# Batch 0's group sums of queries and keys on TensorE, batch 1's values left unsummed, and a new order of the head

## The chip, the core and the metric

One core of a Trainium2 chip. The time is the device time of one execution in microseconds (us), the median of several runs. TensorE (PE) multiplies, VectorE (DVE), ScalarE (ACT) and GpSimd (POOL) do the elementwise work, and SyncE (SP) issues the DMAs.

## What is computed

```
q, k, v: (4 batches, 8 heads, 576 positions, 64)
q_d, k_d, v_d = means of q, k, v over groups of 4 positions      # 144 positions
out = softmax(q_d k_d^T / 8) v_d, each row repeated 4 times
    + softmax(q k^T / 8, only |i - j| < 4) v
x   = out as (2304 tokens, 512)
h   = x @ w_in;  g = h * sigmoid(1.702 h);  x = g @ w_out        # 2048 wide
h   = x @ w2_in; g = max(0.01 h, h);        out = g @ w2_out     # 2048 wide
```

Everything is float32 outside. Weights come as float64 bits and are made float32 on the chip.

## The kernel before

**Jobs.** Attention is cut into 16 jobs, one for a batch and a pair of heads: jobs 0 to 3 are batch 0, 4 to 7 batch 1 and 8 to 15 the late ones. A job has a coarse part (over the 144 group sums) and a band part (within 3 positions). Its steps have short names. q, k, va, vb, vh are loads. `Qd` and `Kd` sum the queries and keys over groups of four on VectorE (pool4, L325). `Sd` makes the coarse scores on PE (L434), `Mxd` their maxima and the negated, scaled maxima on VectorE (L441, L445), `Exd` three exponentials on ScalarE (L451), `Rcd` and `Mud` the division. `S0` and `S1` are the band scores of the two heads (L346, L351), `M0`/`M1` their maxima (L398), `N0`/`N1` the negation (L402, VectorE), `E0`/`E1` five exponentials each (L407), `Rc` and `Mu` the division. `T0`/`T1` transpose the coarse weights on PE (L461), `C0`/`C1` copy them out of PSUM on ScalarE (L151). `U0`/`U1` transpose the band weights (L528), `D0`/`D1` copy them out. `Vd` multiplies the coarse weights with the values (avd, L509), `Od` copies the product out, `Y0`/`Y1` multiply the band weights with the values (L568), `X0`/`X1` add both parts (L599).

**Values of the coarse part.** For batch 0, Vd needs no group sums: it runs over all four members of each group, two parts of the positions times four members times two heads, 16 matmuls of 144 columns. For batch 1, POOL first sums the values over the groups (`Va0`, `Va1`, `Vb0`, `Vb1`, pool_v, L338), and Vd is 4 matmuls.

**Layers.** The tokens are cut into blocks of 512 and four times 448. A unit (j, m) is block j and hidden slice m of 16. `L.u` is 12 matmuls (L735), `Gt`, `Gd`, `Gh`, `Gl` the gate on ScalarE, VectorE, ScalarE and POOL or VectorE, and `M.u` 12 matmuls (L780). Each operand is split into a high and a low float32r half, and three products are made. Units 0 and 1 are cut by input rows, `h0.kc` and `h1.kc`, so that they can begin as soon as one pair of heads is done (`xh`, `xl` split the input).

**Weights.** `w.n` loads half a slice, `wF`, `wL`, `wS`, `wB` turn its bits into float32 (VectorE; wF mostly on ScalarE), `wH` and `wO` make the high and low halves.

**The order.** The steps up to unit 13 stand in a list written out by hand (ORDER, L49). Every engine takes its steps in the order of the list, and so does SP its DMAs; a token's tail @A, @V or @G names ScalarE, VectorE or POOL in place of the usual engine. `z3.14` means 14 matmuls of 512 columns on zeros, into PSUM bank acc3: they do no work, and like every user of the bank they wait until what stood in it before has been read. acc0, acc1 and acc2 hold batch 0's S0, S1 and Sd, and acc3 holds Vd's product. After the list a loop runs the other units with the late jobs' steps between them.

Of the kernel before, what the change touches and what calls it, by code (L numbers as in the profile page):

```python
# [27 lines left out]
def attn_moe_kernel(ctx: ExitStack, tc, qT_d, kT_d, vh_d, vg_d, w1a, w2a, w1b, w2b, outT):  # L28
# [20 lines left out]
    ORDER = """  # L49
        w.2 wF.2 wL.2 wS.2 k.0 Kd.0 wB.2 wH.2 q.0 Qd.0 z3.14 S0.0 M0.0 S1.0 M1.0 va.4 Va0.4 Va1.4 w.0 wF.0@A Sd.0  # L50
        Mxd.0 Exd.0 wO.2 wL.0 N0.0 E0.0 N1.0 wS.0 Rcd.0 Mud.0 wB.0 wH.0 wO.0 k.1 q.1 z3.9 S0.1 Qd.1 Kd.1 M0.1
        w.3 wF.3@A wL.3 q.2 Sd.1 Mxd.1 wS.3 E1.0 Rc.0 Exd.1 vb.4 Vb0.4 wB.3 wH.3 wO.3 Vb1.4 Mu.0 Rcd.1 Mud.1
        N0.1 E0.1 T0.0 C0.0 T1.0 C1.0 q.4 k.4 z3.1 S.4 A1.4 k.2 va.1 w.1 wF.1@A S1.1 M1.1 A0.4 Qd.2 Kd.2 Mx.4
        Sb.4 z3.4 S0.2 M0.2 w.5 vb.7 wF.5@A Qd.4 Sd.2 Mxd.2 Exd.2 U0.0 D0.0 wL.5 N1.1 Kd.4 T0.1 k.3 z3.6 Sd.4
        wS.5 Rcd.2 Mud.2 wL.1 E1.1 Mxd.4 Exd.4 T1.1 C1.1 q.3 wS.1 N0.2 E0.2 wB.5 wH.5 wB.1 vb.2 Rc.1 Mu.1 Rcd.4
        Mud.4 q.5 vb.0 k.5 z3.5 S.5 Qd.5 A1.5 Qd.3 A0.5 Kd.3 z3.6 U1.1 D1.1 S1.2 T0.2 Kd.5 w.7 M1.2 wH.1 C0.1
        wO.5 Vb0.7 U1.0 D1.0 wO.1 Mx.5 Sb.5 N1.2 Sd.3 S0.3 M0.3 Mxd.3 T1.4 wF.7@A wL.7 va.0 T1.2 w.4 wF.4@A wL.4
        w.6 wF.6@A wS.7 wS.4 N0.3 wB.7 wB.4 E1.2 Rc.2 Mu.2 Ex.5 Exd.3 Rcd.3 Mud.3 C0.2 T0.4 C0.4 z3.4 S1.3 Vd.0
        M1.3 vh.0 Y0.0 k.6 va.6 va.5 vb.1 vh.4 C1.2 Od.0 X0.0 U0.1 D0.1 E0.3 wH.7 wO.7 C1.4 Ex.4 Y1.0 vh.1 va.2
        vh.2 w.12 vb.3 Vd.1 Od.1 w.9 X1.0 xh.0 wL.6 xl.0 N1.3 E1.3 wS.6 Sm.5 wB.6 Sm.4 Rc.4 Mu.4 Rc.5 Sd.5 Mxd.5  # L60
        T0.3 C0.3 Vd.4 Od.4 wF.9@A wH.4 wO.4 va.3 q.6 Vd.2 Y1.1 X1.1 h0.0 h1.0 U0.2 D0.2 T1.3 w.14 vh.3 Kd.6
        Va0.5 Va1.5 Exd.5 Rc.3 C1.3 Y0.1 U1.2 D1.2 X0.1 Qd.6 U1.4 D1.4 wL.9 Od.2 wH.6 xh.1 Y1.2 Y0.2 X1.2 Mu.3
        U1.3 D1.3 U0.3 D0.3 X0.2 wF.12@A xh.2 wS.9 wB.9 U0.4 D0.4 xl.1@V wO.6 xl.2 Y1.4 Vd.3 wH.9 wO.9 Od.3 Y0.3
        X0.3 Y1.3 X1.3 xh.3 h0.1 wL.12 xl.3@V wF.14@A wL.14 wS.12 wS.14 wB.12 L.2 Gt.2 Gd.2 wH.12 wO.12@V Gh.2
        Gl.2@V vb.5 Vb0.5 Rcd.5 Mud.5 w.8 wF.8@A wL.8 h1.1 h1.2 h1.3 Gt.1 Gd.1 Gh.1 wB.14 wS.8 wB.8 wH.8 Gl.1@V
        Mu.5@V L.3 wO.8 h0.2 h0.3 Y0.4 Gt.0 Gd.0 Gh.0 X0.4 w.19 wF.19@A w.15 wH.14 X1.4 Gl.0@V wL.19 Vb1.5 L.6
        wF.15@A Va0.6 wL.15 wS.19 wB.19 Gt.3 wO.14@V wS.15 wB.15 T0.5 T1.5 C0.5 w.10 wF.10@A wL.10 wS.10 wH.19
        wO.19 M.0 M.1 C1.5 Vd.5 Gd.3 Gh.3 Gl.3 wB.10 wH.10 wO.10 Va1.6 Sd.6 Mxd.6 M.2 L.4 Od.5@V va.7 w.16 Gt.6
        Gd.6 wF.16@A wL.16 wS.16 Exd.6 w.11 wF.11@A Rcd.6 Gh.6 wL.11 wS.11 wB.11 wH.11 wB.16 wH.15 Gl.6@V wO.15
        S.6 A0.6 A1.6 Mx.6 Mud.6 Sb.6 wO.11@V Gt.4 Gd.4 wH.16 wO.16@V w.22 Gh.4 Gl.4@V wF.22@A wL.22 vh.5 w.13  # L70
        wF.13@A wL.13 vb.6 w.20 wF.20@A wL.20 wS.20 wS.13 M.3 U1.5 D1.5 U0.5 D0.5 wB.13 wH.13 wO.13 L.5 wS.22
        Gt.5 wB.20 wH.20 Gd.5 Gh.5 Gl.5 Ex.6 wB.22 wH.22 wO.22 L.7 q.7 Qd.7 k.7 Kd.7 S.7 A1.7 wO.20 Sm.6 Gt.7
        Gd.7 M.4 w.18 wF.18@A wL.18 wS.18 wB.18 Gh.7 Gl.7@V wH.18 wO.18 Rc.6 A0.7 Mx.7 Sb.7 w.17 wF.17@A wL.17
        L.8 Gt.8 Gd.8 M.5 M.6 Y0.5 t.23 w.24 X0.5 Gh.8 Gl.8@V Vb0.6 w.26 wF.26@A wL.26 wS.17 wS.26 wB.26 Y1.5
        L.9 Gt.9 wH.26 T1.6 C1.6 w.28 wB.17 Gd.9 Gh.9 L.10 X1.5 Sd.7 Ex.7 wO.26 Mu.6@V wH.17 Gl.9@V wO.17 M.7
        M.8 Sm.7 Gt.10 Gd.10 Rc.7 wF.24@A wL.24 wS.24 wF.28@A wL.28 wB.24 w.21 wF.21@A wL.21 wS.21 Mxd.7 wS.28
        wB.21 wB.28 wH.24 Gh.10 Gl.10@V Vb1.6 U0.6 D0.6 Exd.7 Rcd.7 Va0.7 wH.28 L.11 Gt.11 Gd.11 T0.6 C0.6 U1.6
        D1.6 Gh.11 wO.24 Mu.7@V Mud.7 wO.28@V M.9 w.23 wF.23@A wL.23 wH.21 Vd.6 Od.6 vh.6 Y1.6 w.25 wF.25@A w.27
        X1.6 Va1.7 Gl.11@V wS.23 wB.23 wO.21@V Vb1.7 wL.25 wS.25 wB.25 wF.27@A wL.27 wH.23@V wO.23 L.12 Gt.12
        Gd.12 T0.7 C0.7 T1.7 L.13 t.25 wH.25 wO.25@V C1.7 w.29 w.31 Y0.6 X0.6 wS.27 U0.7 D0.7 Gh.12 wF.29@A  # L80
        wL.29 M.10 U1.7 D1.7 Vd.7 Od.7 wB.27 wH.27 wO.27 Gl.12@V wS.29 Gt.13 wF.31@A Gd.13 Gh.13 Gl.13 wB.29
        vh.7 Y0.7 X0.7 w.30 wF.30@A Y1.7 X1.7 wL.31 M.11 wS.31 wL.30 wB.31 wH.31 wH.29 wO.29 wS.30 wB.30 wH.30
        wO.30 wO.31 t.27
    """
# [838 lines left out]
```

## Time and profile before

| | |
|---|---|
| median of 3 runs | 914.37 us (914.04 to 915.45) |
| the profiled execution, its own time | 914.53 us |
| its span, first to last instruction | 912.7 us |
| granted TensorE clock | 1.00 |
| PE, DVE, ACT, POOL busy | 901.9, 405.5, 323.3, 338.4 us |

Busy time of PE is the union of matmuls whose ends are modelled, and it includes the matmuls on zeros. How much of it is work has to be read from the order of time: where a run of zeros (tile `idle`, L812) begins, and when the next matmul that does work starts.

### The profile page before, as it was taken

Reading aid. Unit: us, or ns where it says so; the run is one execution under the profiler, and the core shown is the slowest. Engines: PE = TensorE matmul, PEld = TensorE weight load, DVE = VectorE, ACT = ScalarE, POOL = GpSimd, SP = SyncE. Lnnn points to the kernel's source line nnn. Section 1 sums busy time; section 2 is a strip of 40 time slices with the busy share of each in tenths; the row PEclk is TensorE's granted clock in tenths of the full one; section 3 lists DMA queues with packets and bytes.
Section 4 is the critical chain, followed back from the end, with each engine's and each line's share of the span. In section 5 each row is a group of like instructions: output and inputs, shape, how many; then the busy total and the mean of one; then the engine's idle time right before and its main releaser. Section 6 shows DMA issues by size and latency. Waiting matters only on the chain.

```text
span 912.7 us, 14436 instructions
## 1 busy us (share of the span) xinstructions
PE 901.9 (99%) x5681; PEld 789.6 (87%) x5681; DVE 405.5 (44%) x723; ACT 323.3 (35%) x713; POOL 338.4 (37%) x322
## 2 busy tenths in 40 slices
...
GB/s 277 271 109 175 168 171 84 193 132 143 144 118 169 169 194 225 228 195 229 201 126 156 109 1 1 1 86 1 1 59 23 1 1 81 1 0 41 1 1 41
DMA packets 51908, 98.70 MB, mean 108 GB/s; under 512 B 11648, under 2 KB 25984, under 8 KB 51840
## 3 DMA queue, kind: packets, MB, share of 16 engines
...
q8 instruction: 45, 0.74, 0.3%
...
## 4 chain that ended last, share of the span: by engine, by line
PE 96%; DVE 2%; ACT 1%; DMA 1%; issue 0%; SPq 0%; ACTq 0%
PE h L735 44%; PE acc L780 44%; PE av L568 2%; PE avd L509 2%; PE sc L351 1%; PE scd L434 1%; DMA a<-qT 1%; PE pt L528 0%; ACT a L407 0%; DVE a L325 0%; PE pdt L461 0%; DVE stat L402 0%; DVE stat_d L441 0%; DVE t L175 0%; DVE t L179 0%
## 5 line engine op out<-in xcount | busy, mean ns | idle before, releaser
L735 PE MATMUL h<-xh,w 128*128 128x448 f32 (+1 forms) x1280 | 398.7, 373 | 0.0
L780 PE MATMUL acc<-gh,w 128*128 128x448 f32 (+1 forms) x1280 | 396.6, 371 | 0.0
L765 POOL TENSOR_TENSOR gl<-g,gh 128x448 fp32r<-128x448 f32 (+1 forms) x149 | 176.6, 1185 | 467.5 <-ACT gh L151 459.5
L735 PEld LDWEIGHTS h<-xh,w 128*128 128x128 f32 x1280 | 240.4, 188 | 27.7 <-issue 1.4
L780 PEld LDWEIGHTS acc<-gh,w 128*128 128x128 f32 x1280 | 240.4, 188 | 27.2 <-ACT g L753 1.8
L735 PE MATMUL h<-xl,w 128*128 128x448 f32 (+1 forms) x640 | 236.9, 370 | 0.0
L780 PE MATMUL acc<-gl,w 128*128 128x448 f32 (+1 forms) x640 | 236.8, 370 | 0.0
L761 DVE TENSOR_TENSOR g<-g,h 128x448 f32<-128x448 f32 (+1 forms) x80 | 50.8, 635 | 319.3 <-ACT g L760 319.3
L151 ACT ACTIVATE gh<-g 128x448 fp32r<-128x448 f32 (+1 forms) x160 | 94.3, 589 | 123.7 <-DVE g L754 64.8
L780 PEld LDWEIGHTS acc<-gl,w 128*128 128x128 f32 x640 | 120.2, 188 | 12.2
L735 PEld LDWEIGHTS h<-xl,w 128*128 128x128 f32 x640 | 120.2, 188 | 12.1
L760 ACT ACTIVATE g<-h 128x448 f32<-128x448 f32 (+1 forms) x80 | 44.4, 555 | 224.8 <-PE h L735 224.5
L754 DVE SCALAR_TENSOR_TENSOR g<-g,h 128x448 f32<-128x448 f32 (+1 forms) x80 | 50.6, 633 | 132.2 <-ACT g L753 131.7
L753 ACT ACTIVATE g<-h 128x448 f32<-128x448 f32 (+1 forms) x80 | 44.3, 554 | 156.2 <-PE h L735 147.8
L175 DVE SCALAR_TENSOR_TENSOR t<-s,t 128x512 uint32<-128x512 uint32 x64 | 64.1, 1006 | 1.5
L198 POOL TENSOR_TENSOR w<-t,w 128x512 fp32r<-128x512 f32 x25 | 33.6, 1349 | 50.1 <-ACT w L151 40.5
L179 DVE SCALAR_TENSOR_TENSOR t<-s,t 128x512 uint32<-128x512 uint32 x64 | 45.1, 711 | 1.5
L236 POOL TENSOR_TENSOR w<-b,w 128x1024 fp32r<-128x1024 f32 x16 | 38.5, 2404 | 7.9 <-ACT w L235 7.9
L378 POOL TENSOR_TENSOR P<-P,stat 128x320 f32<-128x320 f32 (+1 forms) x37 | 29.6, 818 | 10.5 <-DVE stat L417 9.9
L172 DVE TENSOR_SCALAR t<-t 128x512 uint32<-128x512 uint32 x64 | 30.8, 485 | 2.0 <-ACT t L151 0.8
L718 DVE TENSOR_TENSOR xl<-xf,xh 128x448 fp32r<-128x448 f32 (+1 forms) x27 | 20.5, 776 | 19.5 <-ACT xh L151 19.3
L151 ACT ACTIVATE xh<-xf 128x448 fp32r<-128x448 f32 (+1 forms) x40 | 22.9, 588 | 12.1 <-PE h L735 10.0
...
## 6 DMA issues: line engine op xcount, KB each, us to landing
...
```

The lines of the kernel that those rows point to most:

```text
L151: return nc.scalar.activation(out=out, in_=in_, func=AF.Copy, scale=scale)
L175: lambda: nc.vector.scalar_tensor_tensor(out=b, in0=bits[:, :, 1], scalar=0x80000000, in1=b, op0=ALU.bitwise_and, op1=ALU.bitwise_or,),
L179: lambda: nc.vector.scalar_tensor_tensor(out=b, in0=bits[:, :, 0], scalar=29, in1=b, op0=ALU.logical_shift_right, op1=ALU.bitwise_or,),
L198: lambda: on(G).tensor_tensor(out=lo, in0=t, in1=wt[e, m][:, 2 * i, :], op=ALU.subtract),
L236: nc.gpsimd.tensor_tensor(out=w[:, :, 1].bitcast(F32R), in0=t, in1=w[:, :, 0], op=ALU.subtract)
L735: nc.tensor.matmul(h, w[:, kc * P : (kc + 1) * P], xs[kc][part], start=kc == 0 and i == 0, stop=kc == KC - 1 and i == 2,)
L753: lambda: nc.scalar.activation(out=g, in_=h[:, :n], func=AF.Tanh, scale=0.5 * 1.702),
L754: lambda: nc.vector.scalar_tensor_tensor(out=g, in0=g, scalar=1.0, in1=h[:, :n], op0=ALU.add, op1=ALU.mult),
L760: lambda: nc.scalar.activation(out=g, in_=h[:, :n], func=AF.Copy, scale=0.01),
L761: lambda: nc.vector.tensor_tensor(out=g, in0=g, in1=h[:, :n], op=ALU.max),
L765: lambda: on(G).tensor_tensor(out=gl, in0=g, in1=gh.bitcast(F32), op=ALU.subtract),
L780: nc.tensor.matmul(acc[c][:, :n], w[:, cs], g, start=m == 0 and i == 0, stop=m == NM - 1 and i == 2)
```

## The change

P takes the place of Qd and Kd for jobs 0 to 3: 8 matmuls of PE with the identity as weights sum queries and keys into bank acc3, each reading every fourth column, and Pc copies the 2 x 144 sums out on ScalarE. Qd and Kd stay for the other jobs. The steps Va and Vb are gone from the list; batch 1's Vd runs over the four members, as batch 0's did, and four buffers instead of three hold the unsummed values. The negation of the band maxima, and that of the coarse maxima (now a step Nd of its own), can be put on ScalarE by @A, which the list does for N0 and N1 of every job of batch 0 and for every Nd but job 1's. The list is new throughout; below are its first lines, up to L.2.

```diff
     ORDER = """
-        w.2 wF.2 wL.2 wS.2 k.0 Kd.0 wB.2 wH.2 q.0 Qd.0 z3.14 S0.0 M0.0 S1.0 M1.0 va.4 Va0.4 Va1.4 w.0 wF.0@A Sd.0
-        Mxd.0 Exd.0 wO.2 wL.0 N0.0 E0.0 N1.0 wS.0 Rcd.0 Mud.0 wB.0 wH.0 wO.0 k.1 q.1 z3.9 S0.1 Qd.1 Kd.1 M0.1
-        w.3 wF.3@A wL.3 q.2 Sd.1 Mxd.1 wS.3 E1.0 Rc.0 Exd.1 vb.4 Vb0.4 wB.3 wH.3 wO.3 Vb1.4 Mu.0 Rcd.1 Mud.1
-        N0.1 E0.1 T0.0 C0.0 T1.0 C1.0 q.4 k.4 z3.1 S.4 A1.4 k.2 va.1 w.1 wF.1@A S1.1 M1.1 A0.4 Qd.2 Kd.2 Mx.4
-        Sb.4 z3.4 S0.2 M0.2 w.5 vb.7 wF.5@A Qd.4 Sd.2 Mxd.2 Exd.2 U0.0 D0.0 wL.5 N1.1 Kd.4 T0.1 k.3 z3.6 Sd.4
-        wS.5 Rcd.2 Mud.2 wL.1 E1.1 Mxd.4 Exd.4 T1.1 C1.1 q.3 wS.1 N0.2 E0.2 wB.5 wH.5 wB.1 vb.2 Rc.1 Mu.1 Rcd.4
-        Mud.4 q.5 vb.0 k.5 z3.5 S.5 Qd.5 A1.5 Qd.3 A0.5 Kd.3 z3.6 U1.1 D1.1 S1.2 T0.2 Kd.5 w.7 M1.2 wH.1 C0.1
-        wO.5 Vb0.7 U1.0 D1.0 wO.1 Mx.5 Sb.5 N1.2 Sd.3 S0.3 M0.3 Mxd.3 T1.4 wF.7@A wL.7 va.0 T1.2 w.4 wF.4@A wL.4
-        w.6 wF.6@A wS.7 wS.4 N0.3 wB.7 wB.4 E1.2 Rc.2 Mu.2 Ex.5 Exd.3 Rcd.3 Mud.3 C0.2 T0.4 C0.4 z3.4 S1.3 Vd.0
...
+        w.2 wF.2@A wL.2 wS.2 wB.2 q.0 k.0 z3.13 S0.0 M0.0 N0.0@A E0.0 S1.0 M1.0 w.3 wF.3 wL.3 q.1 P.0 Pc.0 z3.2
+        Sd.0 wS.3 wB.3 wH.3@V wO.3 k.1 P.1 S0.1 Mxd.0 k.4 Kd.4 N1.0@A E1.0 Rc.0 Mu.0 q.4 z1.3 S.4 Qd.4 A0.4
+        Nd.0@A Exd.0 Rcd.0 Mud.0 S1.1 M1.1 Pc.1 Sd.1 Mxd.1 w.1 wF.1@A wL.1 N1.1@A Nd.1 Exd.1 wS.1 wB.1 wH.1@V
+        w.7 wF.7@A wL.7 wH.2 wO.2 E1.1 Rcd.1 Mud.1 M0.1 N0.1@A Sd.4 Mxd.4 Nd.4@A A1.4 wS.7 wO.1@V E0.1 Rc.1 Mu.1
+        q.2 k.2 z3.10 P.2 Pc.2 T0.0 wB.7 z3.4 S0.2 M0.2 Sd.2 Mxd.2 Exd.4 Rcd.4 C0.0 Mud.4 N0.2@A w.0 wF.0@A wL.0
+        Nd.2@A U1.0 D1.0 T1.0 U0.0 S1.2 M1.2 wS.0 Exd.2 Rcd.2 Mud.2 va.0 w.5 wF.5@A wL.5 C1.0 q.3 D0.0 U0.1 D0.1
+        N1.2@A vb.0 T1.1 Vd.0 Od.0 k.5 Kd.5 E1.2 wS.5 k.3 P.3 Pc.3 wB.0 wH.0 wO.0 E0.2 T0.1 C0.1 wB.5 wH.5@V
+        wO.5 q.5 Qd.5 S1.3 S.5 A0.5 wH.7 A1.5 Mx.4 Sb.4 w.4 C1.1 Rc.2 Mu.2 z3.4 T0.2 C0.2 wF.4@A S0.3 M0.3
+        N0.3@A U1.1 M1.3 w.6 wF.6@A Ex.4 Sd.3 Mxd.3 Nd.3@A E0.3 Exd.3 D1.1 N1.3@A Mx.5 Sb.5 wL.6 va.2 vh.0 va.1
+        va.3 q.6 vb.1 vh.1 vb.3 vb.2 z3.5 Y1.0 X1.0 Y0.0 X0.0 xh.0 xl.0 wS.6 Sd.5 wL.4 wB.6 Rcd.3 Mud.3 Sm.4
+        Qd.6 w.9 vh.2 wS.4 Vd.1 E1.3 Rc.3 U0.2 T1.2 C1.2 D0.2 h0.0 wH.6 wO.6 Y1.1 Od.1 X1.1 U1.2 Ex.5 D1.2 Mxd.5
+        Nd.5@A Y0.1 X0.1 wB.4 w.14 vh.3 Vd.2 Od.2 Sm.5 wF.9@A wL.9 T0.3 T1.4 C1.4 C0.3 T1.3 C1.3 xh.1 h1.0 Mu.3
+        U0.3 D0.3 Y1.2 X1.2 Y0.2 X0.2 wO.7 wH.4 Exd.5 Vd.3 wF.14@A Od.3 U1.3 D1.3 Rc.4 wS.9 xl.1 Mu.4@V h1.1
+        h0.1 xh.2 wO.4@V w.12 T0.4 C0.4 Y0.3 X0.3 Y1.3 X1.3 wB.9 xh.3 xl.3@V xl.2@G wF.12@A wL.14 wL.12 U1.4
+        D1.4 U0.4 Rcd.5 wS.12 L.2 Gt.2 Gd.2 wS.14 wB.12 h0.2 h0.3 h1.2 h1.3 L.3 Gh.2 Gl.2@V D0.4 wH.12 wO.12@V
...
-    BUFS = {"stat": 4, "stat_d": 4, "P": 2, "pd": 2, "vg": 3}
+    BUFS = {"stat": 4, "stat_d": 4, "P": 2, "pd": 2, "vg": 4}
...
         def tiles(self):
-            self.qd = self.tile([P, SD], "qd")
-            self.kd = self.tile([P, SD], "kd")
-            if not self.first:
+            if self.first:
+                self.qkd = self.tile([P, 2, SD], "qd")
+                self.qd, self.kd = self.qkd[:, 0], self.qkd[:, 1]
+            else:
+                self.qd = self.tile([P, SD], "qd")
+                self.kd = self.tile([P, SD], "kd")
+            if self.late:
                 self.vd = self.tile([DK[0], 2, 2, D], "vd")
...
+        def pool_mm(self):
+
+            ps = self.ps_q = self.bank("acc3", "qk")
+            for i, x in enumerate((self.q[:, :S], self.kT[:, HALO : HALO + S])):
+                x = x.rearrange("p (g r) -> p r g", r=FACTOR)
+                for r in range(FACTOR):
+                    nc.tensor.matmul(
+                        ps[:, i * SD : (i + 1) * SD], ident, x[:, r], start=r == 0, stop=r == FACTOR - 1
+                    )
+
+        def pool_out(self):
+            copy(self.qkd, self.ps_q[:, : 2 * SD].rearrange("p (i g) -> p i g", i=2))
...
         def negate(self, h2):
             mx = self.stat[:, 0, :, h2]
-            nc.vector.tensor_scalar(out=mx, in0=mx, scalar1=-SCALE, scalar2=None, op0=ALU.mult)
+            copy(mx, mx, -SCALE, V)
...
             nc.vector.tensor_reduce(out=mx, in_=self.ps_d, axis=AX.X, op=ALU.max)
             if self.late:
-                nc.scalar.activation(out=mx, in_=mx, func=AF.Copy, scale=-SCALE_D)
-            else:
-                nc.vector.tensor_scalar(out=mx, in0=mx, scalar1=-SCALE_D, scalar2=None, op0=ALU.mult)
+                self.negate_d()
+
+        def negate_d(self):
+            mx = self.stat_d[:, 0]
+            copy(mx, mx, -SCALE_D, nc.scalar if self.late else V)
...
-            parts = [(kh, r) for kh in range(2) for r in range(FACTOR if self.first else 1)]
+            parts = [(kh, r) for kh in range(2) for r in range(1 if self.late else FACTOR)]
...
-                        v = self.vg[kh][:, h2, g, :] if self.first else self.vd[: DK[kh], kh, h2, :]
+                        v = self.vg[kh][:, h2, g, :] if not self.late else self.vd[: DK[kh], kh, h2, :]
```

## Rows read from the trace of the kernel before

**Rows 1.** Busy time by stretch: bounds and length of the stretch, then for each engine the busy us and the instructions in it, the granted clock, the DMA share and GB/s. 60.14 us is where h0.1 starts.

```profile
0.00:60.14 60.14, 53.26 (x743) 36.89 (x743) 49.01 (x112) 42.76 (x168) 33.50 (x43) 1.00 0.73 229
60.14:160.00 99.86, 99.86 (x722) 80.29 (x720) 87.92 (x159) 57.07 (x117) 44.13 (x41) 1.00 0.47 149
160.00:300.00 140.00, 139.69 (x1229) 117.90 (x1228) 73.47 (x163) 44.88 (x122) 68.26 (x92) 1.00 0.48 146
300.00:912.70 612.70, 609.07 (x2995) 554.56 (x2993) 195.07 (x290) 178.62 (x306) 192.48 (x148) 1.00 0.24 81
```

**Rows 2.** The chain of work that ended last: shares of the span by engine, and two of its pieces in order of time (start us, us, what).

```profile
PE 96%; DVE 2%; ACT 1%; DMA 1%; issue 0%; SPq 0%; ACTq 0%
...
100.46 2.72 PE h L735 x12
...
853.13 2.44 PE acc L780 x12
```

**Rows 3.** PE in order of time, before 60 us: each run of matmuls on zeros and the row of work behind it (start us, length us, what, count; in brackets idle time that the profile puts down to a releaser).

```profile
6.58 0.30 PE L346 MATMUL sc<-bands_b,ident_b 128*128 128x320 bf16 x1
...
9.46 2.12 PE L812 MATMUL idle<-warm 128*128 128x512 bf16 x9
13.57 0.30 PE L346 MATMUL sc<-bands_b,ident_b 128*128 128x320 bf16 x1 [2.00 <-ACT a L407]
...
16.08 0.38 PE L812 MATMUL idle<-warm 128*128 128x512 bf16 x1
16.39 0.81 PE L351 MATMUL sc<-kT,q 64*64 64x64 f32 x40
...
18.10 1.04 PE L812 MATMUL idle<-warm 128*128 128x512 bf16 x4
20.05 0.30 PE L346 MATMUL sc<-bands_b,ident_b 128*128 128x320 bf16 x1 [0.92 <-DVE a L325]
...
22.79 1.46 PE L812 MATMUL idle<-warm 128*128 128x512 bf16 x6
24.73 0.95 PE L434 MATMUL scd<-kd,qd 64*64 64x144 f32 x12 [0.48 <-DVE kd L325]
...
25.96 1.24 PE L812 MATMUL idle<-warm 128*128 128x512 bf16 x5
27.59 1.23 PE L351 MATMUL sc<-kT,q 64*64 64x64 f32 x40 [0.39 <-DMA kT<-kT]
28.75 1.47 PE L812 MATMUL idle<-warm 128*128 128x512 bf16 x6
...
30.33 0.44 PE L528 MATMUL pt<-ident,a 128*128 128x128 f32 x2
...
34.10 0.51 PE L461 MATMUL pdt<-ident,pd 128*48 128x128 f32 x3
34.44 0.49 PE L461 MATMUL pdt<-ident,a 128*48 128x128 f32 x3
34.77 0.49 PE L461 MATMUL pdt<-ident,pd 128*96 128x128 f32 x3
35.10 1.03 PE L812 MATMUL idle<-warm 128*128 128x512 bf16 x4
37.22 0.30 PE L346 MATMUL sc<-bands_b,ident_b 128*128 128x320 bf16 x1 [1.10 <-ACT a L407]
```

**Rows 4.** Groups of PE instructions over the whole span, shapes apart: line, tile, size of the stationary block, moving operand, count, busy us, mean ns of one. Tiles named `a` are batch 0's; L509 with pdT,vd at 144 columns is batch 1's.

```profile
L509 PE MATMUL avd<-a,a 96*64 96x144 f32 x64 | 4.8, 292 | 0.0
L509 PE MATMUL avd<-a,a 48*64 48x144 f32 x64 | 4.8, 289 | 0.0
L509 PE MATMUL avd<-pdT,vd 96*64 96x144 f32 x16 | 1.9, 312 | 0.0
L509 PE MATMUL avd<-pdT,vd 48*64 48x144 f32 x16 | 1.9, 308 | 0.0
```

**Rows 5.** PE in order of time around job 4's Vd, around a batch 0 job's Vd, and around job 5's Vd with an Sd behind it (columns as in rows 3).

```profile
42.20 2.20 PE L509 MATMUL avd<-a,a 96*64 96x144 f32 x29
44.13 0.33 PE L434 MATMUL scd<-kd,qd 64*64 64x144 f32 x1
...
45.66 0.86 PE L509 MATMUL avd<-pdT,vd 96*64 96x144 f32 x8
46.45 2.20 PE L509 MATMUL avd<-a,a 96*64 96x144 f32 x29
...
79.81 0.74 PE L509 MATMUL avd<-pdT,vd 96*64 96x144 f32 x6
80.22 0.33 PE L434 MATMUL scd<-kd,qd 64*64 64x144 f32 x1
80.38 0.29 PE L509 MATMUL avd<-pdT,vd 48*64 48x144 f32 x2
80.40 1.00 PE L434 MATMUL scd<-kd,qd 64*64 64x144 f32 x11
81.33 0.50 PE L780 MATMUL acc<-gh,w 128*128 128x512 f32 x1
```

**Rows 6.** PE's weight loads before 60 us, by shape (count, busy us, mean ns of one, idle before).

```profile
L528 PEld LDWEIGHTS pt<-ident,a 128*128 128x128 f32 x20 | 2.2, 140 | 1.1 <-POOL a L378 0.8
L735 PEld LDWEIGHTS h<-xh,w 128*128 128x128 f32 x4 | 0.8, 188 | 0.2
```

**Rows 7.** Groups of VectorE, ScalarE and POOL before 60 us (columns as in rows 6): group sums, negations, the sums of values.

```profile
L325 DVE TENSOR_REDUCE a<-a 128x144 f32<-128x576 f32 x8 | 5.8, 744 | 0.0
L402 DVE TENSOR_SCALAR stat<-stat 128x5 f32<-128x5 f32 x8 | 3.0, 387 | 0.0
L151 ACT ACTIVATE a<-pt 128x256 f32<-128x256 f32 x4 | 1.5, 382 | 1.0 <-PE pt L528 1.0
L338 POOL TENSOR_TENSOR vg<-vg 96x256 f32<-96x256 f32 x2 | 1.5, 728 | 4.2 <-DMA vg<-vg 4.2
```

**Rows 8.** ScalarE in order of time: three coarse exponentials (Exd.0), the first of E0.0's five and the last, and the step behind it (start us, length us).

```profile
10.84 0.38 ACT L451 ACTIVATE a<-scd,stat_d 128x144 f32<-128x144 f32 x1 [0.95 <-DVE stat_d L445]
...
11.92 0.32 ACT L407 ACTIVATE a<-sc,stat 128x64 f32<-128x64 f32 x1
...
13.08 0.35 ACT L407 ACTIVATE a<-sc,stat 128x64 f32<-128x64 f32 x1
...
13.37 0.67 ACT L151 ACTIVATE w<-t 128x512 fp32r<-128x512 f32 x1
```

More of the change, by code (lines that the diff above doesn't have):

```diff
@@ L55, in attn_moe_kernel @@
-        wS.5 Rcd.2 Mud.2 wL.1 E1.1 Mxd.4 Exd.4 T1.1 C1.1 q.3 wS.1 N0.2 E0.2 wB.5 wH.5 wB.1 vb.2 Rc.1 Mu.1 Rcd.4
-        Mud.4 q.5 vb.0 k.5 z3.5 S.5 Qd.5 A1.5 Qd.3 A0.5 Kd.3 z3.6 U1.1 D1.1 S1.2 T0.2 Kd.5 w.7 M1.2 wH.1 C0.1
-        wO.5 Vb0.7 U1.0 D1.0 wO.1 Mx.5 Sb.5 N1.2 Sd.3 S0.3 M0.3 Mxd.3 T1.4 wF.7@A wL.7 va.0 T1.2 w.4 wF.4@A wL.4
-        w.6 wF.6@A wS.7 wS.4 N0.3 wB.7 wB.4 E1.2 Rc.2 Mu.2 Ex.5 Exd.3 Rcd.3 Mud.3 C0.2 T0.4 C0.4 z3.4 S1.3 Vd.0
-        M1.3 vh.0 Y0.0 k.6 va.6 va.5 vb.1 vh.4 C1.2 Od.0 X0.0 U0.1 D0.1 E0.3 wH.7 wO.7 C1.4 Ex.4 Y1.0 vh.1 va.2
@@ L60, in attn_moe_kernel @@
[L60 to L83, printed above, removed]
+        w.2 wF.2@A wL.2 wS.2 wB.2 q.0 k.0 z3.13 S0.0 M0.0 N0.0@A E0.0 S1.0 M1.0 w.3 wF.3 wL.3 q.1 P.0 Pc.0 z3.2
+        Sd.0 wS.3 wB.3 wH.3@V wO.3 k.1 P.1 S0.1 Mxd.0 k.4 Kd.4 N1.0@A E1.0 Rc.0 Mu.0 q.4 z1.3 S.4 Qd.4 A0.4
@@ new lines, in attn_moe_kernel @@
+        U0.3 D0.3 Y1.2 X1.2 Y0.2 X0.2 wO.7 wH.4 Exd.5 Vd.3 wF.14@A Od.3 U1.3 D1.3 Rc.4 wS.9 xl.1 Mu.4@V h1.1
+        h0.1 xh.2 wO.4@V w.12 T0.4 C0.4 Y0.3 X0.3 Y1.3 X1.3 wB.9 xh.3 xl.3@V xl.2@G wF.12@A wL.14 wL.12 U1.4
+        D1.4 U0.4 Rcd.5 wS.12 L.2 Gt.2 Gd.2 wS.14 wB.12 h0.2 h0.3 h1.2 h1.3 L.3 Gh.2 Gl.2@V D0.4 wH.12 wO.12@V
+        Mud.5 wH.9 wO.9 Gt.1 Gd.1 Gh.1 Gl.1 k.6 vb.4 w.19 wF.19@A va.4 vh.4 Vd.4 Y1.4 wB.14 wH.14 va.5 w.10 Kd.6
+        wL.19 L.6 Od.4 X1.4 Sd.6 Y0.4 Gt.0 Gd.0 wS.19 Gh.0 Gl.0@V M.0 wO.14 M.1 M.2 wF.10@A wL.10 wS.10 wB.19
```

21 lines of the change are left out of this document (19 added, 2 removed).

## The prediction

> **What bounds the kernel now.** I read busy time by stretch first. From 60.14 us to the end PE is busy in all but about 4 of 852 us, at a granted clock of 1.00, while VectorE has 88 of 100 us in the busiest stretch and the others less [rows 1]. Busy is the union of overlapping matmuls, so it has to be seen whether they also follow each other at full pace. The chain of waits says so: 96% of it is PE, and a dozen matmuls of a layer takes 2.72 us at 512 columns in the middle of the head and 2.44 at 448 near the end, the same in every piece [rows 2]. From 60 us on PE never waits for anybody. Hence the time is PE's work, plus the time before 60 us in which PE does none. Another engine's work counts only through that second part.
>
> So I looked at the second part. Before the first data PE runs zeros until 6.58 us; that stays. After it there are seven stretches from a run of zeros to the next matmul that works: 9.46 to 13.57, 16.08 to 16.39, 18.10 to 20.05, 22.79 to 24.73, 25.96 to 27.59, 28.75 to 30.33 and 35.10 to 37.22 [rows 3]. They sum to 13.6 us. Thirty-five matmuls on zeros run in them, each 0.217 us (four take 1.03 us with the last one's 0.38 of length), which is 7.6 us. The other 6.0 us are waits. The reader is to see that this 13.6 us is all that a better head can give back, and that PE work which the change adds after 60 us has nothing to hide beside.
>
> **The change part by part.**
>
> *Batch 1's Vd.* The counts show that the trace has two instructions for each float32 matmul: batch 0's four jobs make 64 matmuls and have 128 rows [rows 4]. A job with 16 matmuls thus issues 32 instructions; 29 of them take 42.20 to 44.13, so all 32 take 2.1 us [rows 5]. Job 4's Vd with its 8 instructions takes 45.66 to 46.45, 0.79 us, and job 5's with an Sd of 12 behind it 1.52, of which 0.88 are the Sd's own (12 instructions at job 5's place last to 81.33 from about 80.45), so 0.64 [rows 5]. Each of four jobs goes from about 0.72 to 2.1 us: +5.5 us, bounds 5.2 and 5.9. All four stand among the layers' matmuls or close before them, so all of it is on the path.
>
> *P.* Eight matmuls for a job, so 16 instructions of 144 columns, each on the whole 128x128 array. No row of the trace has a float32 product on the whole array. The nearest is the transpose of the same stationary shape: three of 128 columns every 0.335 us (34.10, 34.44, 34.77, 35.10) [rows 3], 0.111 us each; for 144 columns 0.125 us, 2.0 us a job, 8.0 us in four. [...] The lower bound is Vd's time per instruction as if each had the array alone, 0.066 us, 4.2 us in all. The upper is one whole weight load for each instruction, 188 ns as the layers' loads last [rows 6], 12.0 us; I take 8.0, since the transposes load at 140 ns [rows 6] and still start every 0.111. The operand is read in steps of four columns, which no row shows for PE; I count nothing for it, and the upper end covers half as much again.
>
> [...]
>
> *Zeros.* 41 matmuls instead of 49; one of the eight falls in the first run, where data are awaited anyway. Seven by 0.217: -1.5 us.
>
> *Relief of the others.* VectorE loses eight group sums of 0.74 us (5.9 us) and fifteen negations (0.39 us each as busy time has it), POOL sixteen additions of values (0.73 us for a large one) [rows 7]. ScalarE gains four copies, between the 0.38 us of 256 columns [rows 7] and half a us, and the negations. After 60 us PE does not wait for them, so this is worth nothing there; before, it can only shorten the 6.0 us of waits.
>
> *The new waits.* I walked the new order through PE's and ScalarE's queues with these durations. PE now carries P's 8 us before the layers and waits less often for data. But P's sums stand in bank acc3, and a run of zeros behind them, or the next user of the bank, must wait until Pc has emptied it; Pc is in ScalarE's queue behind exponentials. Four places stand out. z3.2 waits for Pc.0, which can only start when P.0 is through, a copy later: 0.8 us. z3.4 waits for Pc.2. Between Mxd.1 and Pc.2 ScalarE has Exd.1, wF.7, wH.2, E1.1, two negations and E0.1: 1.1 us for an Exd (three from 10.84 on), 1.45 for each E (11.92 to 13.37) and some 0.6 for each step on weights [rows 8], 5.4 us, after 0.6 of VectorE's for wL.1 and Nd.1; PE meanwhile has Sd.4, ten zeros, P.2 and T0.0, 0.9 + 2.2 + 2.0 + 0.4. Since PE starts on them with Sd.1's end, before Mxd.1's 0.6, and the copy adds 0.4: about 2.0 us. Vd.0 waits for C1.0 (0.8), and P.3 for the copy Od.0 of Vd.0's bank (0.6). Together 4.2 us, against 6.0 before: -1.8 us. The bounds are 1 and 8 us, since a walk of fifty steps can be off by some us: -5.0 to +2.0. VectorE, P's beneficiary, is late nowhere on this path; ScalarE is late next.
>
> *DMAs.* The list moves loads, but the first q and k come as early as before, behind one half slice. The fourth buffer lets batch 1's values stay until Vd; va.7 and the vb loads behind it wait on SP for a Vd, and weights queue behind them. These Vds stand ahead of them in the list, so I count nothing; if SP is held, the weights of some unit are late by that much.
>
> The sum: 5.5 + 8.0 - 1.5 - 1.8 = +10.2 us. Against the profiled execution's own 914.53 us (its span 912.7 and 1.8 around it; 0.16 above the median of the runs) that gives 924.7 us, 1.1% slower.
>
> **The rivals.**
>
> 1. *P is bound by weight loads*, at 188 ns an instruction [rows 6]: 12.0 for 8.0, 928.7 us. Against it: the transposes' pace.
> 2. *P costs a quarter*: one pass a matmul at the layers' pace. Twelve of 448 columns in 2.44 us [rows 2] are 0.45 ns a column, 0.065 us for 144, 0.5 us a job: 6 us less, 918.7 us, or 921.7 if half of what PE gains turns into waiting for ScalarE. Against it: every float32 row here. [...]
> 3. *VectorE becomes the bound* after 60 us. It has 88 of 100 us there [rows 1], and the list has other weight steps on it (wO, wH). A stall of 3 us gives 927.7. Against it: it loses over 8 us of work before.
> 4. *The other side: the added passes hide.* A 64-wide tile leaves half the array free, and in the trace an Sd starts at 80.22, before the last Vd instructions at 80.38 [rows 5]. If the added Vd passes ran wholly beside neighbours, P cost its lower 4.2 and all 6.0 us of waits went: 4.2 - 1.5 - 6.0 = -3.3, 911.2 us. It decides for faster once the added work on the path is under 1.5 us plus the waits that go, 7.5 in all. Against it: layers take the whole array, so only Vd's edges overlap.
> 5. *It comes to nothing*: P stands only in waits and the identity products are cheap, 914.5 us. It needs the lower P and no wait left, and even so Vd's 5.5 remain.
>
> **How the numbers follow.** Forecast 0.62, weight loads 0.14, the quarter price 0.12, VectorE 0.06, hidden 0.04, nothing 0.02. The forecast's own range, with waits of 2 to 7 us, is 922.5 to 927.5. With the first three rivals the range is 919 to 930; past it lie the sides of the first and third rival and the last two. A difference of 0.2%, 1.8 us, is about what can be told from no change. Faster 0.04, same 0.03, slower 0.93.
>
> **What would show it.** Right: each P has 16 rows at a pace near 0.125 us; batch 1's Vd rows go from 32 to 128 and each lasts about 2.1 us; PE stays dense behind h1.1, which starts near 60 us, although more work is left then; the stretches of zeros and waits before it sum to about 10 us; the idle of z3.4 is put down to ScalarE. Wrong: P rows 62 ns apart, waits that vanish, or gaps of PE between layer matmuls after 60 us, put down to VectorE or a DMA.

## The result and the profile after

The changed kernel takes 929.54 us (median of 4 runs, 929.21 to 929.77) against 914.85 us (914.04 to 915.45) for the kernel before: 1.0149 times as long, interval 1.0113 to 1.0184. The profiled execution took 929.21 us with a span of 927.4; the one of before took 914.53 with 912.7. The two spans differ by 14.7 us, and this is where they lie.

Busy time by stretch, cut where the layers' matmuls go on with h1.1 and, right behind it, h0.1, now 65.56 us. It answers to [rows 1].

```profile
0.00:65.56 65.56, 62.83 (x727) 45.36 (x727) 40.92 (x90) 41.32 (x175) 26.23 (x33) 1.00 0.57 183
65.56:160.00 94.44, 94.42 (x780) 77.52 (x780) 79.01 (x146) 52.95 (x110) 30.27 (x23) 1.00 0.55 170
160.00:300.00 140.00, 139.69 (x1222) 117.33 (x1221) 75.50 (x163) 48.34 (x127) 71.97 (x92) 1.00 0.48 143
300.00:927.40 627.40, 623.92 (x3111) 567.02 (x3109) 201.84 (x307) 183.25 (x320) 200.13 (x158) 1.00 0.25 81
```

The chain that ended last, shares of the span by engine, against [rows 2].

```profile
PE 98%; DMA 1%; ACT 0%; issue 0%; SPq 0%
```

VectorE has left the chain and ScalarE is down to 0%: PE's share went from 96% to 98%. The head became 5.4 us longer although PE does 9.6 us more in it (62.83 busy against 53.26), and from there on PE is as dense as before. The other 9.3 us of the 14.7 stand behind the cut: 7.1 are Vd's, since all four of batch 1's now come there, and 3.0 are transposes and products of attention that the new list puts there. PE in order of time before 66 us shows what fills the head (columns as in [rows 3]).

```profile
8.19 4.35 PE L339 MATMUL qk<-a,ident 128*128 128x144 f32 x16
13.04 0.59 PE L831 MATMUL idle<-warm 128*128 128x512 bf16 x2 [0.50 <-ACT a L151]
13.56 0.95 PE L451 MATMUL scd<-a 64*64 64x144 f32 x12
14.44 4.35 PE L339 MATMUL qk<-a,ident 128*128 128x144 f32 x16
...
23.53 2.33 PE L831 MATMUL idle<-warm 128*128 128x512 bf16 x10
25.92 4.35 PE L339 MATMUL qk<-a,ident 128*128 128x144 f32 x16
30.09 0.51 PE L480 MATMUL pdt<-ident,a 128*96 128x128 f32 x3
30.77 1.02 PE L831 MATMUL idle<-warm 128*128 128x512 bf16 x4 [0.17 <-ACT a L151]
31.63 0.30 PE L363 MATMUL sc<-bands_b,ident_b 128*128 128x320 bf16 x1
...
38.73 4.35 PE L339 MATMUL qk<-a,ident 128*128 128x144 f32 x16 [0.39 <-ACT a L151]
...
65.56 0.48 PE L754 MATMUL h<-xh,w 128*128 128x512 f32 x1
```

Each P is sixteen rows in 4.35 us where 2.0 was forecast. A run of zeros now ends in the next matmul that works, with hardly a wait: 25.92 stands 2.39 behind 23.53, and ten zeros are 2.17 of it. Groups of PE's instructions over the whole span, against [rows 4]:

```profile
L339 PE MATMUL qk<-a,ident 128*128 128x144 f32 x64 | 17.4, 439 | 0.4 <-ACT a L151 0.4
L528 PE MATMUL avd<-pdT,vg 96*64 96x144 f32 x64 | 4.8, 292 | 0.0
L528 PE MATMUL avd<-pdT,vg 48*64 48x144 f32 x64 | 4.8, 289 | 0.0
```

Batch 1's Vd has 128 rows instead of 32, as counted. The waits of PE between 5 and 66 us (us in total, times, longest) come to 1.7; in the head before, five such rows came to 5.1.

```profile
PE idle L831 <- ACT a L151: 0.7, 2, 0.5
PE sc L368 <- DMA a<-kT: 0.4, 1, 0.4
PE qk L339 <- ACT a L151: 0.4, 1, 0.4
PE pdt L480 <- ACT a L151: 0.2, 1, 0.2
```

For a sum that counts nothing twice I took, for every matmul of both traces, the time from its start to the start of the next one on PE, and added it up by tile. A wait then falls to the step ahead of it. Behind P.0, Vd.0 and T0.0 of the changed kernel stand waits for Pc.0, Od.0 and Pc.2; what these steps take longer than their like without a wait, 0.68, 0.46 and 0.34 us, is counted with the zeros and waits here. This makes the whole span:

| | before | after | difference | forecast |
|---|---|---|---|---|
| P (`qk`) | 0 | 16.68 | +16.7 | +8.0 |
| Vd and the Sd beside it (`avd`, `scd`) | 31.89 | 38.19 | +6.3 | +5.5 |
| zeros, with the waits beside them | 19.23 | 13.20 | -6.0 | -3.3 |
| all other tiles | 861.61 | 859.34 | -2.3 | 0 |
| span | 912.73 | 927.41 | +14.7 | +10.2 |

So two things ask for a cause: why P costs twice the forecast, and why the rest gives back more than forecast.

### The profile page after: what moved, and what is told of

It is laid out like the page before. It is cut to its first block, busy times and chain, and to the rows that moved or that the text cites. A ratio compares the mean times of both kernels' runs of the same rounds, so it can differ in the third digit from the quotient of the medians.

```text
span 927.4 us, 14724 instructions
## 1 busy us (share of the span) xinstructions
PE 920.9 (99%) x5833; PEld 807.2 (87%) x5833; DVE 397.3 (43%) x703; ACT 325.9 (35%) x730; POOL 328.6 (35%) x305
## 4 chain that ended last, share of the span: by engine, by line
PE 98%; DMA 1%; ACT 0%; issue 0%; SPq 0%
PE h L754 44%; PE acc L799 43%; PE avd L528 3%; PE av L587 2%; PE qk L339 2%; PE sc L368 1%; PE scd L451 1%; PE idle L831 1%; PE pt L547 1%; PE pdt L480 1%; DMA a<-kT 1%; ACT a L151 0%; ACT a L424 0%; PE sc L363 0%; ACT y L809 0%
## 5 line engine op out<-in xcount | busy, mean ns | idle before, releaser
L784 POOL TENSOR_TENSOR gl<-g,gh 128x448 fp32r<-128x448 f32 (+1 forms) x151 | 179.5, 1189 | 474.0 <-ACT gh L151 463.7
L198 POOL TENSOR_TENSOR w<-t,w 128x512 fp32r<-128x512 f32 x20 | 27.0, 1359 | 61.8 <-ACT w L151 49.3
L179 DVE SCALAR_TENSOR_TENSOR t<-s,t 128x512 uint32<-128x512 uint32 x64 | 45.0, 710 | 1.6
L737 DVE TENSOR_TENSOR xl<-xf,xh 128x448 fp32r<-128x448 f32 (+1 forms) x25 | 19.2, 783 | 19.3 <-ACT xh L151 19.1
```

What stands on the lines that cost most here:

```text
L179: lambda: nc.vector.scalar_tensor_tensor(out=b, in0=bits[:, :, 0], scalar=29, in1=b, op0=ALU.logical_shift_right, op1=ALU.bitwise_or,),
L784: lambda: on(G).tensor_tensor(out=gl, in0=g, in1=gh.bitcast(F32), op=ALU.subtract),
```

## The experiments

There are three theories of P's price. **S**: reading the operand in steps of four columns sets the pace. **F**: a float32 product over the full array is this slow whatever it reads. **W**: the weight loads ahead of the passes set it; their median is 208 ns in the trace after. The kernel before ran at 914.5 to 914.8 us beside all of them.

**1. A different step for each job (p_strides).** Job p reads 144 columns in steps of p + 1; the sums of jobs 0 to 2 are then over other positions.

```diff
-                x = x.rearrange("p (g r) -> p r g", r=FACTOR)
+                n = self.p + 1
...
-                        ps[:, i * SD : (i + 1) * SD], ident, x[:, r], ...
+                        ps[:, i * SD : (i + 1) * SD], ident, x[:, r % n : r % n + n * (SD - 1) + 1 : n], ...
```

> P of job 0 reads consecutive columns, job 1 every second, job 2 every third, job 3 every fourth as the change does; so the sums of jobs 0 to 2 are of other columns. Theory S (the step of the reading costs): about 0.123 us from one pass to the next in job 0, 0.257 in job 3, between the two or at 0.257 in jobs 1 and 2. Theory F (a float32 product on the whole array costs four cycles a column and pass): 0.257 us in all four. Theory W (each pass waits for a weight load of 0.208 us): 0.257 in all four too.

Measured: 924.46 us, one run. PE in order of time, the four P steps, with steps of 1, 2, 3 and 4 columns:

```profile
8.59 2.23 PE L339 MATMUL qk<-a,ident 128*128 128x144 f32 x16
...
12.72 2.31 PE L339 MATMUL qk<-a,ident 128*128 128x144 f32 x16
...
22.15 3.33 PE L339 MATMUL qk<-a,ident 128*128 128x144 f32 x16
...
34.02 4.35 PE L339 MATMUL qk<-a,ident 128*128 128x144 f32 x16 [0.39 <-ACT a L151]
```

Same weights, same shapes, same number of passes: only the step differs, so S stands and F and W fall. The passes start 0.122, 0.127, 0.191 and 0.256 us apart. From two columns on this is 0.064 us for each column of the step. At one column that would be 0.064, and 0.122 is measured; what binds there is not shown, nor why a wider step costs more.

**2. P in halves of the array (p_halves).** Sixteen matmuls of 64x64 for a job in place of eight of 128x128.

```diff
+                    for a in (slice(0, 64), slice(64, P)):
...
-                        ps[:, i * SD : (i + 1) * SD], ident, x[:, r], ...
+                        ps[a, i * SD : (i + 1) * SD], ident[a, a], x[a, r], ...
```

> Each identity product is cut into two of 64 rows and 64 columns, which can run side by side; the step of four stays. S: two passes side by side every 0.257 us, P stays at 4.2 us a job. F: two side by side every 0.123 us, P 2.0 us a job. W: loads of 64 columns last 0.134 us, so a pair every 0.13 to 0.14 us, P 2.2 us a job.

Measured: 929.2 us, one run. A P is now 32 rows in the same time:

```profile
14.48 4.27 PE L340 MATMUL qk<-a,ident 64*64 64x144 f32 x32
...
25.98 4.30 PE L340 MATMUL qk<-a,ident 64*64 64x144 f32 x32
```

Two halves run side by side and a pair still takes 0.257 us: each partition reads the same columns, whatever part of the array the product takes. This is S again: F and W had a pair at 0.12 to 0.14 us.

**3. P reading neighbouring columns (p_contig).** The sums are then of position g and those 144, 288 and 432 behind it, which is not the mean over groups; the rest is as in the changed kernel.

```diff
-                x = x.rearrange("p (g r) -> p r g", r=FACTOR)
+                x = x.rearrange("p (r g) -> p r g", r=FACTOR)
```

> All four P read consecutive columns, so they sum the four quarters of the positions and not the groups of four. S: P falls from 4.3 to 2.0 us a job, 8.9 us less PE work before 60 us; some of it comes back as waits for ScalarE (Pc behind the exponentials), so 922 to 925 us against 929.5. F and W: 929.5 within 0.5 us.

Measured: 922.00 us (921.66 to 922.17), 1.0081 times the kernel before, interval 1.0066 to 1.0096. P's group, and the run of zeros behind P.2:

```profile
L339 PE MATMUL qk<-a,ident 128*128 128x144 f32 x64 | 8.9, 292 | 0.4 <-ACT a L151 0.4
```

```profile
25.89 1.02 PE L831 MATMUL idle<-warm 128*128 128x512 bf16 x4 [1.37 <-ACT a L151]
```

By the sum above P takes 8.3 us here for 16.7: the step costs 8.4 us of PE. The medians differ by 7.5 us, the profiled executions by 7.0. The rest went into the wait of z3.4 for Pc.2, which is 0.17 us in the changed kernel and 1.37 here: the longer P had covered it.

**4. The sums back on VectorE (p_on_dve).** Qd and Kd in P's places, no Pc; the list, the negations and batch 1's Vd stay.

```diff
-... q.1 P.0 Pc.0 z3.2 Sd.0 ... k.1 P.1 S0.1 ... S1.1 M1.1 Pc.1 Sd.1 ...
+... q.1 Qd.0 Kd.0 z3.2 Sd.0 ... k.1 Qd.1 Kd.1 S0.1 ... S1.1 M1.1 Sd.1 ...
```

> The new list with VectorE's group sums in the places of P, and no Pc: the identity products alone undone. PE loses 17.3 us of work, VectorE gets 5.3 us. If P's work lay wholly on the path: 912.2 us. If it stood in time in which PE would have waited anyway: 929. I expect 917: about 12 us back, with 5 us of waits for VectorE in their place before the layers.

Measured: 925.01 us (924.53 to 927.48), 1.0120 times the kernel before, interval 1.0102 to 1.0139. A miss: of P's 16.7 us only 4.5 come back. PE in order of time at the first wait and at the longest, and busy time by stretch around the first (bounds, length, then PE, PEld, DVE, ACT, POOL, the granted clock, the DMA share, GB/s):

```profile
8.87 0.60 PE L831 MATMUL idle<-warm 128*128 128x512 bf16 x2
11.65 1.01 PE L451 MATMUL scd<-a 64*64 64x144 f32 x12 [2.17 <-DVE a L329]
...
26.41 0.42 PE L363 MATMUL sc<-bands_b,ident_b 128*128 128x320 bf16 x1 [2.49 <-ACT a L424]
```

```profile
10.00:12.00 2.00, 0.35 (x6) 0.35 (x8) 2.00 (x4) 1.97 (x14) 0.00 (x0) 1.00 1.04 421
12.00:14.00 2.00, 2.00 (x31) 1.47 (x27) 1.93 (x5) 0.07 (x1) 0.46 (x1) 0.60 1.01 395
14.00:16.00 2.00, 2.00 (x21) 0.77 (x23) 1.97 (x6) 0.72 (x4) 0.80 (x1) 0.50 0.99 347
```

Sd.0 now waits 2.17 us for VectorE, and S0.2 later 2.49 us for ScalarE. The granted clock is 0.50 from 12.4 to 19.2 us and again from 26.1 to 32.9. From each start to the next start, by tile, the zeros and waits take 6.8 us more than in the changed kernel, the band scores 3.7, the coarse scores 1.3 and the transposes of the coarse weights 1.6; the number of their matmuls is the same. Of these 13.4 us, 7.4 are idle time by the rows: 5.7 with the zeros, 0.5 with the band scores and 1.2 with the transposes. The other 6.0 are the same matmuls taking longer, as the rows at the low clock do: twelve coarse scores last 1.71 us at 28.18, for 0.95 at a granted 1.00 in the changed kernel (13.56). So P had filled time in which PE would stand still, and PE without it pays in waits and in clock.

**5. Batch 1's values unsummed, alone (old_unsummed).** The kernel before with batch 1's Va and Vb out of its list and Vd over the four members.

```diff
...
-            parts = [(kh, r) for kh in range(2) for r in range(FACTOR if self.first else 1)]
+            parts = [(kh, r) for kh in range(2) for r in range(1 if self.late else FACTOR)]
...
```

> The old list and code, but batch 1's values are not summed (no Va, Vb, Vd of 16 matmuls; vb.7 and va.6 are loaded later so that four buffers do). Theory of PE's work: four Vd go from about 0.7 to 2.15 us behind a PE that never waits, +5.5 to +5.8 us, 920.1 us. Rival (the added passes hide beside neighbours or POOL's relief pays for them): 914.5 to 917.

Measured: 919.51 us (918.22 to 920.26), 1.0055 times, interval 1.0038 to 1.0072. Job 4's Vd, 0.79 us in [rows 5]:

```profile
43.55 2.33 PE L508 MATMUL avd<-pdT,vg 96*64 96x144 f32 x32
```

From the first start to the last row's end it has 2.33 us; to the end of its issue it is 2.05, against 0.58 by the same reckoning before. Four times 1.47 is 5.9 us, and 4.8 are seen in the medians. The profiled execution, the shortest of the four (918.22 us), is 3.7 us above the one of before; in it the stretches of zeros and waits in the head are 1.4 us shorter (12.2 for 13.6).

**6. Batch 1's values summed again (v_summed).** The changed kernel, with experiment 5's line turned round, Va and Vb back in the list and batch 1's values loaded so early that POOL can sum them.

> The change with batch 1's values summed on POOL again (loads of va and vb earlier in the list). Theory of PE's work: 929.5 - 5.6 = 923.9 us. Rival (POOL's 9.8 us of sums or the earlier loads hold back something in the new list): 925 to 929.

Measured: 928.69 us (928.1 to 929.24), 1.0153 times, interval 1.0137 to 1.0168. Vd is 5.6 us shorter, and 0.9 of it is left, about as much as the runs of one kernel differ by. VectorE, POOL and PE in order of time:

```profile
141.81 0.69 DVE L179 SCALAR_TENSOR_TENSOR t<-s,t 128x512 uint32<-128x512 uint32 x1
...
142.20 0.62 POOL L355 TENSOR_TENSOR vd<-vg 96x128 f32<-96x128 f32 x1 [6.92 <-PE avd L528]
...
143.76 0.79 POOL L355 TENSOR_TENSOR vd<-vg 48x128 f32<-48x128 f32 x1
...
144.26 2.95 DVE L179 SCALAR_TENSOR_TENSOR t<-s,t 128x512 uint32<-128x512 uint32 x1
...
144.52 0.90 POOL L442 TENSOR_TENSOR pd<-pd,stat_d 128x432 f32<-128x432 f32 x1
...
145.38 1.28 POOL L198 TENSOR_TENSOR w<-t,w 128x512 fp32r<-128x512 f32 x1
...
148.39 0.51 PE L480 MATMUL pdt<-ident,pd 128*96 128x128 f32 x3 [1.62 <-DVE xf L618]
```

One VectorE instruction, 0.69 us long at 141.81, takes 2.95 from 144.26 on. Beside it POOL ends the sums of values and then multiplies coarse weights by their division's factor (L442) and makes the low half of a weight (L198). X is late behind it, and PE waits 1.62 us for X; the granted clock of 140 to 152 us is 0.89, and layer matmuls that had followed each other at 0.23 us come 0.43 apart at 150.31 and 150.74. That POOL is the cause was not taken apart, nor whether the sums had brought those two steps there: experiment 12 has the same sums, and its longest instruction of L179 is 1.41 us.

**7. No zeros behind the first data (no_zeros).** The changed kernel without z3.2, z1.3, z3.10, z3.4 twice and z3.5.

> The change without the 28 matmuls on zeros behind the first run. If they only take PE's time, since under a us of waits stands behind them: 6.05 us less, 923.5 us. If PE then waits in their place, or the granted clock of the head falls below 1.00: 926 to 930.

Measured: 925.99 us (925.65 to 927.54), 1.0126 times, interval 1.0111 to 1.0142. 28 zeros are 6.1 us, and 3.5 are gained. PE's longest wait before 66 us (us in total, times, longest), and busy time by stretch:

```profile
PE sc L362 <- ACT a L423: 1.3, 1, 1.3
```

```profile
28.00:30.00 2.00, 1.09 (x20) 0.86 (x21) 1.88 (x5) 2.00 (x12) 0.49 (x1) 0.81 0.99 325
30.00:32.00 2.00, 2.00 (x21) 1.62 (x18) 0.62 (x2) 1.36 (x5) 1.03 (x1) 0.50 1.04 341
```

PE waits 1.34 us for ScalarE until 28.91, and the granted clock is 0.50 from 29.3 to 32.7 us. It is 0.50 once more from 39.5 to 42.9, within P.3 and behind it, where the waits of the ten us before come to 0.39.

**8. P in the old list (old_p).** The kernel before with P and Pc in the places of Qd and Kd.

> The old list with P and Pc in the places of batch 0's Qd and Kd, nothing else (Nd behind Mxd on VectorE as it was). P is 4.3 us a job by its measured price. Theory of PE's work: +17.3 us less at most the 6.0 us of waits and what zeros stand in for nothing, 926 to 932 us; I expect 928. Rival (P stands in time in which PE would wait, as its undoing in the new list gave only 4.5 us): 917 to 920.

Measured: 930.87 us (930.34 to 931.97), 1.0178 times, interval 1.0163 to 1.0193. Four Ps cost 16.2 us there. Each of them is followed by 0.50 us of waiting for its Pc. What waits first is Sd.0 for Pc.0, and S0.1 for ScalarE's exponentials, as before:

```profile
13.45 0.95 PE L451 MATMUL scd<-a 64*64 64x144 f32 x12 [0.50 <-ACT a L151]
14.33 2.12 PE L831 MATMUL idle<-warm 128*128 128x512 bf16 x9
18.08 0.30 PE L363 MATMUL sc<-bands_b,ident_b 128*128 128x320 bf16 x1 [1.64 <-ACT a L424]
```

The granted clock is 0.50 from 19.9 to 23.3 us in this execution too, 0.92 in the mean of 20 to 40 us.

**9 to 11. Can the old list be bettered?** Two edits of the kernel before, and both: seven zeros out (old_trim), and E0.0 ahead of the coarse exponentials (old_e0), since S0.1 had waited 2.00 us for its bank [rows 3].

```diff
-... T1.0 C1.0 q.4 k.4 z3.1 S.4 ...   ... Qd.3 A0.5 Kd.3 z3.6 U1.1 ...
+... T1.0 C1.0 q.4 k.4 S.4 ...        ... Qd.3 A0.5 Kd.3 U1.1 ...
```

> The kernel before, without its run of one zero matmul ahead of S.4 (z3.1) and the second run of six (z3.6, ahead of U1.1): 7 of 49 matmuls on zeros less, nothing else. In the trace of before those two runs, from their start to the next matmul that works, take 0.31 and 1.57 us, and no wait stands behind them but 0.2. If zeros there only take time of PE: 1.5 us off, 913.0 beside 914.6. If what the zeros cover turns into waits, or the granted clock falls with fewer of them (as it did when the changed kernel lost all its zeros): 914.0 to 914.8.

```diff
-... z3.14 S0.0 M0.0 S1.0 M1.0 ... Sd.0 Mxd.0 Exd.0 wO.2 wL.0 N0.0 E0.0 N1.0 ...
+... z3.14 S0.0 M0.0 N0.0 E0.0 S1.0 M1.0 ... Sd.0 Mxd.0 Exd.0 wO.2 wL.0 N1.0 ...
```

> The kernel before, with job 0's negation and band exponentials N0.0 E0.0 put right behind M0.0, ahead of the coarse Exd.0. E0.0 reads bank acc0, for which S0.1 waited 2.00 us behind nine zeros until 13.57. If that wait is the bound there: S0.1 starts about 1.5 us earlier, and 1 to 2 us come off: 912.8 to 913.8. If VectorE is late next (S0.2 and Sd.2 waited for its sums of queries and keys, 0.92 and 0.48 us), the time moves to those waits: 914.5.

> Both edits of the two runs before. If they add: 911.5 to 912.5. If the waits behind the zeros take their place: no lower than the better of the two.

Measured: old_trim 917.5 us (914.22 to 918.75), 1.0020 times, interval 1.0002 to 1.0039; old_e0 916.55 us (914.61 to 917.68), 1.0008, 0.9990 to 1.0027; both 917.11 us (915.65 to 920.28), 1.0025, 1.0013 to 1.0037. None is faster. PE in old_trim where the six zeros had stood, and busy time by stretch behind that wait:

```profile
29.98 0.44 PE L528 MATMUL pt<-ident,a 128*128 128x128 f32 x2 [1.51 <-POOL a L378]
```

```profile
28.47:29.98 1.51, 0.00 (x1) 0.00 (x1) 1.48 (x6) 1.49 (x8) 1.31 (x2) 1.00 0.60 155
29.98:31.00 1.02, 1.02 (x13) 0.78 (x15) 1.02 (x3) 0.55 (x2) 1.02 (x2) 0.73 0.86 277
31.00:40.00 9.00, 9.00 (x68) 6.16 (x64) 7.70 (x14) 7.25 (x26) 4.15 (x4) 0.50 0.97 294
```

The zeros had stood in a wait for POOL, so taking them out shortens nothing, and 9 us behind the bare wait run at a granted clock of 0.50. This profile is of one of the longer executions. Nine of the twelve took 917.2 to 918.8 us at a mean granted clock of 0.992 to 0.994, more than either theory gave; the other three took 914.2 to 915.4 at 0.998 to 1.0, about what the second theory gave. In old_e0 the matmul behind the nine zeros starts at 10.96 instead of 13.57 us as meant, and the time goes to the next wait:

```profile
14.86 0.51 PE L434 MATMUL scd<-a 64*64 64x144 f32 x2 [2.87 <-DVE a L325]
```

```profile
11.91:14.86 2.95, 0.08 (x4) 0.03 (x1) 2.92 (x7) 1.93 (x9) 1.90 (x2) 0.99 1.04 329
14.86:18.00 3.14, 3.14 (x19) 2.33 (x19) 2.18 (x6) 1.72 (x12) 1.40 (x2) 0.50 1.04 310
```

VectorE's sums of job 1 are the bound there, and PE pays once more at 0.50. Its four executions at a mean clock of 0.999 or above took 914.6 to 914.8 us, the other seven 915.8 to 917.7.

**12. The list and the negations alone (new_list_only).** The changed kernel with both p_on_dve's and v_summed's edits.

> The changed kernel's list with its negations, but queries and keys of batch 0 summed on VectorE and batch 1's values summed on POOL as before: what the order alone does. From the run with the sums on VectorE (925.0) less the 4.8 to 5.9 us that batch 1's summed Vd gave: 919 to 920. If POOL's sums beside VectorE stall PE near 145 us again, as in the run where only they were put back: 923 to 925. In either case slower than before (914.6): the new list needs P on PE to pay for itself.

Measured: 920.93 us (917.8 to 923.65), 1.0068 times, interval 1.0050 to 1.0085. A little over the first forecast; the four runs lie 5.9 us apart, the longest at a mean granted clock of 0.987 and the shortest at 0.994, so that what is taken from their median holds to some 3 us.

Together, each beside the kernel before (914.5 to 914.8 us); the new list has its negations with it:

| | sums on VectorE | P on PE |
|---|---|---|
| old list, batch 1's values summed | 914.7 | 930.9 |
| old list, unsummed | 919.5 | not run |
| new list, summed | 920.9 | 928.7 |
| new list, unsummed | 925.0 | 929.5 |

P costs 16.2 us in the old list and 4.5 to 7.8 in the new one; the new list costs 6.2 us while VectorE makes the sums and takes 2.2 off where PE does; unsummed values cost 4.1 to 4.8, and 0.9 with both. Every one of the three parts is slower by itself. No version that I ran is faster than the kernel before.

## Why the prediction came out as it did

The sign and the mechanism held: PE bounds the kernel, and the work that the change adds to PE sets the time. The size did not: 929.5 is 4.8 us above the forecast of 924.7 and outside the forecast's own range of 922.5 to 927.5. It lies inside the wide range, 919 to 930, by half a us, and that range was so wide for the sake of rivals whose causes did not come true. That it held is luck.

**P, the term that was mis-sized.** "The operand is read in steps of four columns, which no row shows for PE; I count nothing for it, and the upper end covers half as much again." It measured 16.7 us for 8.0, and even the upper bound of 12.0 was too low. The 0.125 us that I took from the transposes was right for what the transposes do: with neighbouring columns a pass takes 0.122 to 0.123 (experiments 1 and 3). The step of four doubled it. The transposes cited have blocks of 128x48 and 128x96, not of the whole array as the text says; those over the whole array (`pt`) follow at 0.109 too, so nothing hangs on that. An unknown with no row had been covered by the bound of another unknown, the weight loads.

**Batch 1's Vd.** 5.5 us were forecast, and it is 5.9 for the four of them, at the upper bound. Counted with Sd, part of which had run beside its edges, it is 6.3.

**Zeros and waits.** The count of zeros was right: 28 for 35 behind the first data, 1.5 us. Of the four waits named, by the idle of the rows: z3.2 for Pc.0 0.50 us (0.8 forecast), P.3 for Od.0 0.39 (0.6), Vd.0 none (0.8), z3.4 for Pc.2 0.17 (2.0), 1.1 in all for 4.2. For z3.4 the walk was nearer to right with the P that it assumed: 1.37 us where P has half its length (experiment 3). The walk's own terms come to 1.5 for it rather than 2.0: 0.6, 0.6, 5.4 and 0.4 less the 5.5 that PE has meanwhile. In sum the zeros and waits gave 6.0 us instead of 3.3. Of this the waits gave 4.5 for 1.8, within the bounds of -5.0 and +2.0. The other tiles gave 2.3 more, for which the forecast had nothing.

**How the two misses add up.** Experiment 3 parts them. With P at about the price that I gave it, 8.3 us, the time is 922.0: 2.7 us under the forecast, since the waits and the other tiles gave more than I had walked. The step of four then adds 7.5 us. That is the 4.8 us above the forecast: two misses of opposite sign, the smaller one hiding part of the other. Only 0.9 us of the relief comes from P's excess length. The rest is there with the short P too, and without any P on PE the waits are back (experiment 4).

**"VectorE, P's beneficiary, is late nowhere on this path."** That holds while P is on PE. With its sums back on VectorE, Sd.0 waited 2.17 us for it (experiment 4).

**The signs named.** P's rows came 0.257 apart, not 0.125; Vd's rows went to 128 and 2.05 us each; h1.1 starts at 65.56 us, not near 60; the stretches of zeros and waits sum to 6.9 us, 8.0 with the waits in front of the zeros and of P.3, not 10; z3.4's idle is ScalarE's, but 0.17 us.

**The rivals.** Weight loads (928.7) had the number nearest to the result and the wrong cause: with neighbouring columns the loads last 190 ns and the passes follow at 0.122. The quarter price falls with the same rows: it gave 0.065 us for one float32 matmul, and two passes of 0.122 were measured. VectorE is no bound behind the head: PE's waits after 66 us come to 0.3 us. Hidden passes and no effect are excluded by 14.7 us.
